# Sinkhorn on 128 partitions with a block matmul for the column sums, and float32 loading of one batch's values

## The chip, the cores and the metric

The kernel runs on one core of one Trainium2 chip. The metric is the device time of one execution, in microseconds (us). The kernel before takes 251.91 us (median of three runs, 251.24 to 252.35).

Engine names, as the profile has them: PE is TensorE (PEld is its weight load), DVE is VectorE, ACT is ScalarE, POOL is GpSimd, SP is SyncE. A "q" behind a name is that engine's sequencer, which issues transfers. Shapes in the profile are partitions x elements: the kernel's on-chip tiles have up to 128 rows, called partitions. Every instruction carries the line of the kernel's source, so the same operation has different line numbers in different kernels; the text says which is which.

## The reference

Two stages follow each other. The first is a block-sorted attention: four batches, eight heads, 768 positions, head dimension 64. The positions form eight blocks of 96. A small matrix for every batch and head is normalised by five Sinkhorn rounds and then mixes the blocks of the keys and of the values:

```python
P = sort_net                                   # (4, 8, 8, 8)
for _ in range(5):
    P = np.exp(P - P.max(-1, keepdims=True))
    P = P / (P.sum(-1, keepdims=True) + 1e-9)  # row sums
    P = P / (P.sum(-2, keepdims=True) + 1e-9)  # column sums
k_sorted = np.einsum('bhij,bhjcd->bhicd', P, k_blocks)
v_sorted = np.einsum('bhij,bhjcd->bhicd', P, v_blocks)
attn = softmax(q_block @ k_sorted_block.T / 8)      # inside each block
x    = attn @ v_sorted                              # -> (3072, 512)
```

The second stage is a gated feed-forward block on these 3072 rows, with weights of 512x1536, 512x1536 and 1536x512:

```python
out = (silu(x @ w_gate) * (x @ w_val)) @ w_out
```

## The kernel before

The feed-forward matmuls are the mass of the work, and they keep TensorE busy once batch 0's attention has delivered the first rows. Until then there is a start-up: Sinkhorn, value mixing ("tv"), key mixing ("tkq"), scores ("qk"), attention times values ("av_ps"), and then the first gate matmul ("g_ps"). The change and the argument touch this start-up.

```python
# loads: all of q, k, v on GpSimd, which casts float32 to bfloat16 on the way
load_v(0, 0, HC); load_v(0, HC, C)             # batch 0's values, two halves of columns
make_identity(nc, ident)
load_q(0, 0, C)
for lo, hi in ((0, 32), (32, 64), (64, 80), (80, 96)):
    load_k(0, lo, hi)
copy_v(nc.gpsimd, 0, lowr, 0)                  # transposing copies of the values into vch
copy_v(nc.gpsimd, 0, lowr, 3)
landed = const.tile([R, 1], BF16)
nc.gpsimd.tensor_copy(landed, kq_tiles[0][0:R, C - 1, D - 1:D])   # waits for the last key piece
# ... then the weight loads ...

# Sinkhorn on 32 partitions (batch, head) x 64 elements; all sums on DVE, Exp on ACT
for it in range(N_ITER):
    nc.scalar.activation(p_ps, p_sb if it == 0 else p_ps, AF.Exp)
    # ... it 2 and 3: one transposing value copy on ACT behind the Exp ...
    nc.vector.reduce_sum(rowred[:, :, 0], p_ps, axis=AX.X)
    nc.vector.reciprocal(rowred, rowred)
    nc.vector.tensor_mul(p_ps, p_ps, rowred.to_broadcast([BH, NB, NB]))
    nc.vector.reduce_sum(colred[:, 0, :], p_ps.transpose([0, 2, 1]), axis=AX.X)
    nc.vector.reciprocal(colred, colred)
    if it < N_ITER - 1:
        nc.vector.tensor_mul(p_ps, p_ps, colred.to_broadcast([BH, NB, NB]))
# ... two expansions to p_bf, then 16 small matmuls ("weights") spread P over 128 partitions ...
mix_of(0, w_ps)                                # masks it into vmix and rmix (bfloat16)

# filling matmuls keep TensorE active meanwhile; their results are not used
for _ in range(114): ...                       # 32 columns each
fill(idle_ps, 6)                               # 512 columns each, released by the first values
nc.tensor.matmul(idle_ps[0:NB, 0:NB], lhsT=hold, rhs=hold, ...)   # released by ACT in round five
fill(idle_ps, 5)

def v_chunk(b, at, n, eng, tag):               # value mixing
    ...
    for ld in range(n):
        nc.tensor.matmul(tp[:, ld, :], lhsT=vch[rows, col:col + 128], rhs=mix, start=True, stop=True)
    drain(eng, ...)
# 64 such matmuls, then 192 of key mixing (kq_chunk), then qk, av, transposes, gate
```

The softmax here doesn't subtract the row's maximum and nothing guards it: scores larger than these inputs give would overflow.

## Time and profile before

The first profile of the kernel before fell into a slow state (an execution far above the fastest of the same kernel). The second line below has each engine's busy time, share of the span and number of instructions, TensorE first. Page of the kernel before, first profile:

```profile
span 621.8 us, 6025 instructions
PE 606.0 (97%) x2542; PEld 269.0 (43%) x2568; DVE 165.1 (27%) x342; ACT 113.0 (18%) x187; POOL 51.6 (8%) x46
```

A span of 621.8 us is not that of the timed executions of 251.9; the profiled one took 623.76. The prediction had only this page. The unchanged kernel was therefore profiled again as the first experiment (b_again). From here on "before" means this profile. The page of the kernel before, profiled again; PEclk is the granted clock of TensorE in tenths, in 40 equal slices of the span:

```profile
span 250.0 us, 6051 instructions
PE 240.3 (96%) x2568; PEld 143.2 (57%) x2568; DVE 159.4 (64%) x342; ACT 110.7 (44%) x187; POOL 51.8 (21%) x46
PEclk9999999999999999999999999999999999999999
```

The same profile by stages. The columns are: stretch, its length, busy time of PE, PEld, DVE, ACT and POOL with instruction counts, then the granted clock, DMA share and GB/s:

```profile
0.00:12.70 12.70, 8.48 (x145) 5.09 (x146) 8.62 (x45) 8.23 (x12) 10.07 (x15) 1.00 0.81 157
12.70:20.50 7.80, 7.62 (x262) 6.01 (x263) 6.34 (x8) 5.38 (x8) 4.28 (x7) 1.00 0.69 103
20.50:25.30 4.80, 4.50 (x82) 2.93 (x83) 4.12 (x14) 3.94 (x8) 3.14 (x5) 1.00 1.27 159
25.30:250.00 224.70, 219.71 (x2080) 129.18 (x2079) 140.27 (x277) 93.11 (x161) 34.35 (x20) 1.00 0.50 91
```

The rows are Sinkhorn, mixing, scores and attention, and the dense part. A clock of 1.00 in the first row says little: time without a clock record counts as full, and the record starts at 8.29 us.

### The profile page before, as it was taken

Reading aid. Unit: us, or ns where it says so; the run is one execution under the profiler, and the core shown is the slowest. Engines: PE = TensorE matmul, PEld = TensorE weight load, DVE = VectorE, ACT = ScalarE, POOL = GpSimd, SP = SyncE. Lnnn points to the kernel's source line nnn. Section 1 sums busy time; section 2 is a strip of 40 time slices with the busy share of each in tenths; the row PEclk is TensorE's granted clock in tenths of the full one; section 3 lists DMA queues with packets and bytes.
Section 4 is the critical chain, followed back from the end, with each engine's and each line's share of the span. In section 5 each row is a group of like instructions: output and inputs, shape, how many; then the busy total and the mean of one; then the engine's idle time right before and its main releaser. Section 6 shows DMA issues by size and latency. Waiting matters only on the chain.

```text
span 621.8 us, 6025 instructions
## 1 busy us (share of the span) xinstructions
PE 606.0 (97%) x2542; PEld 269.0 (43%) x2568; DVE 165.1 (27%) x342; ACT 113.0 (18%) x187; POOL 51.6 (8%) x46
## 2 busy tenths in 40 slices
PE   7999999999999999999999999999999999999997
PEld 4754545544444444544434343334334433333323
DVE  5433333322332322223223122123113112212200
ACT  5331212121021111222102201102112111110100
POOL 6675000600000000000000000000000000000000
DMA  7999920000006000000100000001000000000001
GB/s 153 149 208 211 180 16 2 1 18 17 1 17 105 15 17 1 17 1 23 31 6 23 24 13 17 18 13 31 17 16 14 17 16 14 17 17 0 18 30 38
DMA packets 37866, 23.98 MB, mean 39 GB/s; under 512 B 26064, under 2 KB 34000, under 8 KB 37328
## 3 DMA queue, kind: packets, MB, share of 16 engines
q0 software_dynamic: 21328, 14.16, 15.5%
q1 hardware_dynamic: 16512, 9.45, 5.5%
q8 instruction: 20, 0.33, 0.2%
q14 instruction: 6, 0.05, 0.0%
HBM read 28.32 MB, written 7.86 MB: 58 GB/s over the span
## 4 chain that ended last, share of the span: by engine, by line
PE 97%; issue 2%; DVE 0%
PE v_ps L376 27%; PE g_ps L358 27%; PE o_ps L393 25%; PE tkq L237 3%; PE av_ps L307 3%; PE qk L280 2%; PE idle_ps L419 2%; PE tv L249 2%; PE tv L259 2%; PE x_ps L324 1%; PE o_ps L409 1%; PE idle_ps L422 1%; PE g_ps L506 1%; PE v_ps L506 0%; PE w_ps L435 0%
## 5 line engine op out<-in xcount | busy, mean ns | idle before, releaser
L376 PE MATMUL v_ps<-xt,wv_sb 128*128 128x384 bf16 x380 | 190.7, 686 | 0.0
L358 PE MATMUL g_ps<-xt,wg_sb 128*128 128x384 bf16 x376 | 188.9, 683 | 0.0
L393 PE MATMUL o_ps<-wo_sb,h 128*128 128x512 bf16 x255 | 161.3, 832 | 7.7 <-issue 7.7
L368 DVE SCALAR_TENSOR_TENSOR gs_sb<-th_sb,g_ps 128x384 bf16<-128x384 bf16 x96 | 52.9, 551 | 251.1 <-ACT th_sb L366 251.1
L358 PEld LDWEIGHTS <-wg_sb 128*128 128x128 bf16 x376 | 64.1, 176 | 86.9 <-issue 86.5
L376 PEld LDWEIGHTS <-wv_sb 128*128 128x128 bf16 x380 | 60.9, 165 | 93.5 <-issue 93.2
L366 ACT ACTIVATE th_sb<-g_ps 128x384 bf16<-128x384 f32 x96 | 47.2, 491 | 257.2 <-PE g_ps L358 252.4
L393 PEld LDWEIGHTS <-h 128*128 128x128 bf16 x276 | 47.1, 174 | 98.8 <-issue 98.7
L381 DVE SCALAR_TENSOR_TENSOR h<-v_ps,gs_sb 128x384 bf16<-128x384 f32 x96 | 52.5, 547 | 63.0 <-PE v_ps L376 62.9
L398 ACT COPY o_sb<-o_ps 128x512 f32<-128x512 f32 x23 | 13.5, 586 | 158.7 <-PE o_ps L393 158.7
L307 PEld LDWEIGHTS <-e_all 96*128 96x128 bf16 x256 | 26.2, 153 | 17.1 <-issue 16.5
L120 POOL COPY vch<-v 64x1536 bf16<-64x1536 bf16 (+1 forms) x10 | 27.7, 2807 | 57.4 <-PE tv L249 53.9
L307 PE MATMUL av_ps<-vt,e_all 96*128 96x65 bf16 x256 | 27.6, 287 | 0.3 <-PE x_ps L324 0.3
L293 ACT ACTIVATE e_all<-qk 96x768 bf16<-96x768 f32 x30 | 22.6, 802 | 28.7 <-PE qk L280 28.7
L313 DVE TENSOR_TENSOR st<-av_ps,r_sb 96x512 bf16<-96x512 f32 x32 | 21.7, 680 | 0.2
L311 DVE RECIPROCAL r_sb<-av_ps 96x8 f32<-96x8 f32 x32 | 6.5, 203 | 49.3 <-PE av_ps L307 49.3
L237 PE MATMUL tkq<-rmix,kq 128*64 128x64 bf16 x384 | 14.9, 271 | 1.0 <-issue 1.0
L237 PEld LDWEIGHTS <-kq 128*64 128x64 bf16 x384 | 13.7, 183 | 4.8 <-issue 4.7
L215 DVE CAST vt<-tv 96x1024 bf16<-96x1024 f32 (+1 forms) x9 | 9.9, 1105 | 14.1 <-PE tv L249 7.4
L419 PE MATMUL idle_ps<-warm_sb 128*128 128x512 bf16 x19 | 12.5, 795 | 0.7 <-issue 0.3
L217 ACT CAST vt<-tv 96x1024 bf16<-96x1024 f32 (+1 forms) x9 | 9.2, 1026 | 18.3 <-PE tv L259 11.7
L324 PEld LDWEIGHTS <-st 96*128 96x128 bf16 x64 | 8.8, 170 | 7.2 <-issue 7.2
(79 smaller groups left out, 200.2 us busy)
## 6 DMA issues: line engine op xcount, KB each, us to landing
out_dram<-o_sb SPq DMA_DIRECT2D x23, 256.0 KB, 2.0
v<-in_v_dram POOLq DMA_DIRECT2D x3, 768.0 KB, 19.6
kq<-in_q_dram POOLq DMA_DIRECT2D x2, 768.0 KB, 14.1
wg_sb<-in_moe_w_gate_dram POOLq DMA_DIRECT2D x6, 256.0 KB, 8.4
wv_sb<-in_moe_w_val_dram POOLq DMA_DIRECT2D x6, 256.0 KB, 9.1
wo_sb<-in_moe_w_out_dram POOLq DMA_DIRECT2D x1, 1536.0 KB, 25.3
kp<-in_k_dram POOLq DMA_DIRECT2D x2, 768.0 KB, 14.9
q_scr<-in_q_dram POOLq DMA_DIRECT2D x2, 768.0 KB, 28.6
```

What stands on the lines that cost most here:

```text
L120: eng.tensor_copy(dst, src.transpose([0, 2, 1]))
L237: nc.tensor.matmul(tp[two * D:(two + 1) * D, lc, :], lhsT=kq_tiles[b][:, at + lc, :], rhs=rm[:, two, :], start=True, stop=True)
L293: nc.scalar.activation(e_all[:, n:n + 2, 0:4 * C], wide[0:C, :, 0:4 * C], AF.Exp, scale=scale)
L307: nc.tensor.matmul(o[:, two, i4, :], lhsT=e[:, i4 * C:i4 * C + 128], rhs=vt[:, 2 * g + two, half * 4 + i4, :], start=True, stop=True)
L313: nc.vector.tensor_tensor(st.rearrange("p i two d -> p two i d"), o[0:C, :, :, 0:D], r_sb.to_broadcast([C, 2, 4, D]), op=ALU.mult)
L358: nc.tensor.matmul(g_ps, lhsT=wg_sb[:, kc, ts(m, 128)], rhs=xt[:, kc, :], start=(kc == 0), stop=(kc == NKC - 1))
L366: nc.scalar.activation(th_sb, g_ps, AF.Tanh, scale=0.5)
L368: nc.vector.scalar_tensor_tensor(gs_sb, th_sb, 1.0, g_ps, op0=ALU.add, op1=ALU.mult)
L376: nc.tensor.matmul(v_ps, lhsT=wv_sb[:, kc, ts(m, 128)], rhs=xt[:, kc, :], start=(kc == 0), stop=(kc == NKC - 1))
L381: nc.vector.scalar_tensor_tensor(h_tiles[n][:, m, :], v_ps, 0.5, gs_tiles.pop(m), op0=ALU.mult, op1=ALU.mult)
L393: nc.tensor.matmul(o_ps, lhsT=h_w[:, m, ts(t3, 128)], rhs=wo_sb[:, m, :], start=(m == 0), stop=(m == NFC - 1))
L419: nc.tensor.matmul(tile, lhsT=warm_sb[:, 0:128], rhs=warm_sb, start=True, stop=True)
```

## The change

The intent is to shorten the Sinkhorn chain and its end, and to take work off GpSimd:

1. P stands on 128 partitions (pair of batches, head, row) with 16 elements each. Row sums stay on DVE; column sums come from one float32 matmul with a block-diagonal matrix of ones.
2. The last round yields the mixing matrix through one multiply, two matmuls with a selection matrix, a reciprocal and one masked write, in place of two expansions, 16 matmuls and two masked writes. One matrix now serves values and keys; for this, batch 1's queries and keys swap halves of the partitions.
3. Batch 0's values come as float32 in four pieces on SyncE, not as a cast to bfloat16 on GpSimd. The transposing copies do the cast.
4. The weight loads wait for an earlier key piece.
5. Four units of batch 1 are transposed by DMA, not by PE.
6. The filling matmuls are arranged anew, around the block matmuls.

```diff
-    p_sb = const.tile([BH, NB, NB], FP32)
-    nc.sync.dma_start(out=p_sb, in_=sn)
+    p_sb = const.tile([128, NP, NB], FP32)
+    nc.scalar.dma_start(out=p_sb, in_=sn)
+    blk = const.tile([128, 128 // NB, NB], FP32)          # block-diagonal ones
@@
+    v0_tiles = []
+    for half in range(2):
+        t = kqp.tile([128, HC * D + 16], FP32, name=f"v0_{half}", tag="kqt")
+        t = t[0:H * NB, 0:HC * D].rearrange("p (c d) -> p c d", d=D)
+        for part in range(2):
+            c0 = half * HC + part * QC
+            nc.sync.dma_start(out=t[:, part * QC:(part + 1) * QC], in_=v_nat[0, :, c0:c0 + QC, :])
+        v0_tiles.append(t)
@@
-    load_v(0, 0, HC)
-    load_v(0, HC, C)
@@
-    copy_v(nc.gpsimd, 0, lowr, 0)
-    copy_v(nc.gpsimd, 0, lowr, 3)
+    copy_v0(nc.gpsimd, 0, 0, 24)
+    copy_v0(nc.gpsimd, 1, 20, 28, 0, 32)
+    copy_v0(nc.gpsimd, 1, 20, 28, 32, 32)
@@  the round
+        nc.scalar.activation(e_ps, p_sb if it == 0 else a_ps, AF.Exp)
+        # it 1, 2, 3: value copies on ACT, behind the Exp
+        nc.vector.reduce_sum(rows_sb[:, :, 0], e_ps, axis=AX.X)
+        nc.vector.reciprocal(rows_sb, rows_sb)
+        nc.vector.tensor_mul(x_sb, e_ps, rows_sb.to_broadcast([128, NP, NB]))       # float32
+        nc.tensor.matmul(c_ps..., lhsT=blk_flat, rhs=x_sb..., start=True, stop=True)
+        dots(32) if it < 2 else fill(idle_ps, 4)                                    # filling matmuls
+        nc.vector.reciprocal(c_ps, c_ps)
+        nc.vector.tensor_mul(a_ps, x_sb, c_ps)
@@  units of batch 1
-                if b < 2:
+                if b == 0 or b == 1 and u < H2:
```

(The fill and dots line is drawn together from four lines.)

## The prediction

> **What bounds the kernel now.** The only profile of before fell in a slow state: span 621.8 us against 251.9 us timed, PE busy 97% with a 384-column matmul every 0.43 to 0.50 us. I trust its DVE, ACT and DMA durations and rescale PE. [...]
>
> **Start-up, from the timeline of before.** Exp starts at 2.40 us; one Sinkhorn round is 1.7 us (six DVE ops 0.22 to 0.26 us apart, one Exp of 0.19). The chain ends at 10.9, two expansions reach 11.64, then come 16 small matmuls and one multiply (0.21). In the profile these matmuls wait behind slow warm-up matmuls until 13.87; at full clock I estimate the first value-mixing matmul at 12.7 us. It also needs the last ACT transposing copy, which ends at 12.61, so two paths are level.
>
> **What the change does.**
> 1. A round loses one reduction (0.24 us), its ops shrink from 64 to 16 elements (estimated 0.05 us each), but gains a float32 block matmul with two engine hops. I assume 0.4 us for it (nothing in this trace is float32): 1.7 to 1.9 us a round, no gain or a small loss. Exp may start 0.3 us later (finer load, issued on ACT before its table load).
> 2. The end is shorter: no expansions (0.74), no 16 matmuls, one mix instead of two. Instead: one multiply of 128 elements, matmul, reciprocal, mix: about 1.3 us after the last row sum against about 2.2.
> 3. Batch 0's values arrive as float32 on SyncE, freeing 1.19 us of GpSimd issue and letting copies start earlier; ACT has no copies after 11.5 us. I expect value mixing to start near 11.9 us: gain 0.8 us.
> 4. Weight loads no longer wait for the last key piece (before: 4.6 us wait, ending 16.63). They start perhaps 1 us earlier; not critical by itself, but it keeps the stream ahead (output weights land at 57 us in before).
> 5. Four units of batch 1 use DMA instead of PE transposes: 16 fewer. In the slow trace four take 0.43 us; at full clock I estimate 0.06 to 0.08 us each, about 1.1 us off the dense PE stage, plus four 0.36 us DVE copies that cost nothing. DMA transposes land in 2.3 us, well before use.
>
> **Sum.** 0.8 + 1.1 = about 2 us. Predicted 250.0 us; eight times in ten 248.0 to 251.9. Faster by over 2%: 0.06; within 2%: 0.92; slower: 0.02.
>
> **What would show it.** First value-mixing matmul at 11.5 to 12.3 us (before, in the same state, 12.7); 0.3 to 0.6 us between the DVE multiply and the next reciprocal; rounds of 1.7 to 1.9 us; ACT's last transposing copy before 11.6; weight issues starting near 15.5; 16 fewer PE transposes, four more DMA ones, PE not waiting for them.
>
> **What would make it wrong.** A float32 matmul well over 0.6 us, times five, would eat the gain. Warm-up matmuls before each block matmul could delay it if the clock is low, or thinner filling could leave PE slow during value and key mixing (cost 2 to 3 us). Float32 values landing late would block ACT's copies and, behind them, the next Exp. If start-up is bound by key loads rather than the chain, item 3 yields nothing.

Cut from the first paragraph is a TensorE rate that no trace had shown, with the split that rested on it: about 30 of the 252 us for a start-up in which PE waits, and dense PE work for the rest. The forecast's sum, 0.8 + 1.1 = about 2 us, loses no term by the cut.

## More of the kernel before

Timeline of the kernel before, in its start-up. Columns: start in us, duration, engine, line, operation, what it writes and reads, count; in brackets the idle time of the engine just ahead and what ended it:

```profile
6.09 5.62 POOL L120 COPY vch<-v 64x1536 bf16<-64x1536 bf16 x2 [0.48 <-DMA v<-in_v_dram]
7.73 0.19 ACT L187 ACTIVATE p_ps<-p_ps 32x64 f32<-32x64 f32 x1
9.40 0.19 ACT L187 ACTIVATE p_ps<-p_ps 32x64 f32<-32x64 f32 x1
9.61 2.97 ACT L118 COPY vch<-v 64x768 bf16<-64x768 bf16 x2
12.09 0.21 DVE L445 TENSOR_TENSOR vmix<-mask,w_ps 64x64 bf16<-64x64 bf16 x1 [0.53 <-PE w_ps L435]
12.72 2.02 PE L249 MATMUL tv<-vmix,vch 64*128 64x64 bf16 x64
14.73 1.33 PE L237 MATMUL tkq<-rmix,kq 128*64 128x64 bf16 x64
20.50 0.69 PE L280 MATMUL qk<-kqt 64*128 64x96 bf16 x24
25.26 0.48 PE L506 MATMUL g_ps<-xt,wg_sb 128*128 128x384 bf16 x2
```

Two Exp stand 9.40 − 7.73 = 1.67 us apart: that is one Sinkhorn round. Two paths end together: the mixing matrix is written from 12.09 on, and ACT's last value copy ends at 9.61 + 2.97 = 12.58. Value mixing starts at 12.72, behind both. The first gate matmul starts at 25.26; this is the number to watch.

## The result, and the profile after

The changed kernel takes 259.29 us (median of four runs, 259.03 to 259.89); the kernel before took 252.03 in the same rounds (251.24 to 252.35). The ratio is 1.0296, with a 95% interval of 1.0266 to 1.0327. A ratio here is the mean time of one kernel's fast runs over the mean of the other's fast runs of the same rounds, so it is not quite the ratio of the medians. The result is slower by more than 2%, outside the predicted range.

The page of the changed kernel, and then the stages:

```profile
span 257.0 us, 6031 instructions
PEclk9986999999999999999999999999999999999999
0.00:16.90 16.90, 9.81 (x151) 7.00 (x153) 7.23 (x42) 7.38 (x11) 8.65 (x16) 1.00 0.86 187
16.90:27.20 10.30, 9.40 (x259) 8.32 (x263) 6.43 (x8) 5.48 (x7) 9.56 (x13) 0.67 0.88 109
27.20:32.50 5.30, 4.28 (x81) 2.86 (x83) 3.65 (x11) 4.01 (x8) 2.23 (x5) 1.00 1.51 212
32.50:257.00 224.50, 217.95 (x2043) 128.71 (x2063) 139.29 (x273) 92.86 (x161) 31.57 (x16) 1.00 0.47 88
```

Read against the four stages of before, the whole loss lies ahead of the dense part: 4.2 us in the Sinkhorn stage (16.9 against 12.7), 2.5 in mixing (10.3 against 7.8, at a clock of 0.67), 0.5 behind it. The dense part takes 224.5 us against 224.7. (The four DMA transposes do save about 1 us there, but in this profile PE also stands idle for 1.06 us from 68.64 on, a stall of a kind that comes up again below.)

Timeline of the changed kernel, the lines that answer to those of before:

```profile
5.97 0.50 PEld L240 LDWEIGHTS chain<-x_sb,blk 128*128 128x128 f32 x2 [0.66 <-issue]
6.00 0.58 PE L240 MATMUL chain<-x_sb,blk 128*128 128x16 f32 x2 [0.58 <-DVE x_sb L239]
6.62 0.27 DVE L253 RECIPROCAL chain<-chain 128x16 f32<-128x16 f32 x1 [0.57 <-PE chain L240]
7.72 1.05 ACT L141 CAST vch<-v 64x512 bf16<-64x512 f32 x1 [2.48 <-DMA v<-in_v_dram]
8.68 0.16 ACT L227 ACTIVATE chain<-chain 128x16 f32<-128x16 f32 x1
10.79 0.17 ACT L227 ACTIVATE chain<-chain 128x16 f32<-128x16 f32 x1 [0.56 <-DVE chain L254]
12.91 0.17 ACT L227 ACTIVATE chain<-chain 128x16 f32<-128x16 f32 x1 [0.47 <-DVE chain L254]
14.55 0.28 DVE L266 SCALAR_TENSOR_TENSOR rmix<-f_ps,cinv,mask 64x64 bf16<-64x64 f32 x1
15.16 3.36 POOL L143 CAST vch<-v 64x896 bf16<-64x896 f32 x2 [6.53 <-DMA v<-in_v_dram]
16.89 3.57 PE L313 MATMUL tv<-rmix,vch 64*128 64x64 bf16 x64 [2.31 <-POOL vch L143]
20.39 1.92 PE L301 MATMUL tkq<-rmix,kq 128*64 128x64 bf16 x64
27.21 0.69 PE L344 MATMUL qk<-kqt 64*128 64x96 bf16 x24
32.47 0.48 PE L527 MATMUL g_ps<-xt,wg_sb 128*128 128x384 bf16 x2 [0.24 <-ACT xt L281]
```

Four things can be read from it.

- Value mixing waits for values. At 16.89 it starts after waiting 2.31 us for GpSimd's copies, and those began at 15.16 after waiting 6.53 us for the last piece of the load.
- The chain itself was held up by values. ACT's copy waited 2.48 us for a piece and began at 7.72. The Exp behind it in ACT's program had been released by DVE's result (ended at 7.10), but started only at 8.68.
- A round takes 2.12 us where nothing disturbs it (12.91 − 10.79), not 1.67. The float32 matmul appears as two matmuls with two weight loads.
- Value mixing takes 3.57 us, not 2.02, and the first 64 key-mixing matmuls 1.92, not 1.33. The clock record has half clock from 17.1 to 23.9 us; in before it is full from 8.3 us to the end.

The view of transfers, up to 20 us, has the load itself. Columns: what, issuing queue, count, KB each, median time from issue to landing. First before, then the changed kernel:

```profile
v<-in_v_dram POOLq DMA_DIRECT2D x2, 384.0 KB, 5.4
```

```profile
v<-in_v_dram SPq DMA_DIRECT2D x4, 384.0 KB, 6.8
```

The bytes written are twice as many. The trace's landing events are plainer than the medians: before, the two pieces land at 6.04 and 7.94 us; after, the four pieces land at 5.80, 7.69, 9.38 and **15.03**. The queries landed at 12.42 before and 14.68 after.

The records of the single packets show the sharing directly. In the changed kernel the values wrote 223 KB/us from 3.0 to 7.2 us, with no queries beside them. The first packet of the queries started at 7.20, when 80 of the values' 256 packets had not started. At the old rate these 80 would have ended near 9.4 us (an estimate: 80 x 6,144 bytes / 223 KB/us = 2.2 us); the last one ended at 13.68.

### The profile page after: what moved, and what is told of

It reads as the page before. It is cut to its first block, busy times and chain, and to the rows that moved or that the text cites. A ratio compares the mean times of both kernels' runs of the same rounds, so it can differ in the third digit from the quotient of the medians.

```text
span 257.0 us, 6031 instructions
## 1 busy us (share of the span) xinstructions
PE 241.4 (94%) x2532; PEld 146.9 (57%) x2558; DVE 156.6 (61%) x332; ACT 109.7 (43%) x186; POOL 52.0 (20%) x47
## 4 chain that ended last, share of the span: by engine, by line
PE 83%; DMA 5%; DVE 4%; issue 3%; ACT 2%; SPq 1%; POOL 1%; DVEq 0%; ACTq 0%; POOLq 0%
PE v_ps L440 23%; PE g_ps L422 22%; PE o_ps L457 22%; DMA v<-in_v_dram 5%; PE tkq L301 4%; PE av_ps L371 3%; PE qk L344 2%; PE tv L313 2%; PE tv L323 1%; DVE gs_sb L432 1%; DVE st L377 1%; PE o_ps L473 1%; ACT e_all L357 1%; DVE h L445 1%; PE x_ps L388 1%
## 5 line engine op out<-in xcount | busy, mean ns | idle before, releaser
L440 PE MATMUL v_ps<-xt,wv_sb 128*128 128x384 bf16 x380 | 77.3, 326 | 0.3
L422 PE MATMUL g_ps<-xt,wg_sb 128*128 128x384 bf16 x376 | 76.5, 325 | 0.0
L457 PE MATMUL o_ps<-wo_sb,h 128*128 128x512 bf16 x255 | 61.9, 379 | 1.2 <-issue 0.2
L440 PEld LDWEIGHTS <-wv_sb 128*128 128x128 bf16 x380 | 35.7, 97 | 24.1 <-issue 1.4
L422 PEld LDWEIGHTS <-wg_sb 128*128 128x128 bf16 x376 | 34.5, 97 | 22.7
L457 PEld LDWEIGHTS <-h 128*128 128x128 bf16 x276 | 26.2, 98 | 28.2
L371 PEld LDWEIGHTS <-e_all 96*128 96x128 bf16 x256 | 12.2, 98 | 5.0 <-ACT e_all L357 0.9
L371 PE MATMUL av_ps<-vt,e_all 96*128 96x65 bf16 x256 | 13.5, 194 | 0.3 <-ACT e_all L357 0.2
L279 DVE CAST kqt<-tkq 128x1024 bf16<-128x1024 f32 (+1 forms) x7 | 7.5, 1071 | 4.4 <-PE tkq L301 3.8
L281 ACT CAST kqt<-tkq 128x1024 bf16<-128x1024 f32 (+1 forms) x7 | 6.1, 891 | 8.1 <-PE tkq L301 8.1
```

The lines of the kernel that those rows point to most:

```text
L279: nc.vector.tensor_copy(dst, src)
L371: nc.tensor.matmul(o[:, two, i4, :], lhsT=e[:, i4 * C:i4 * C + 128], rhs=vt[:, 2 * g + two, half * 4 + i4, :], start=True, stop=True)
L422: nc.tensor.matmul(g_ps, lhsT=wg_sb[:, kc, ts(m, 128)], rhs=xt[:, kc, :], start=(kc == 0), stop=(kc == NKC - 1))
L440: nc.tensor.matmul(v_ps, lhsT=wv_sb[:, kc, ts(m, 128)], rhs=xt[:, kc, :], start=(kc == 0), stop=(kc == NKC - 1))
L457: nc.tensor.matmul(o_ps, lhsT=h_w[:, m, ts(t3, 128)], rhs=wo_sb[:, m, :], start=(m == 0), stop=(m == NFC - 1))
```

## The experiments

The theory: (T1) the float32 load lands late and holds up both the chain (through ACT) and value mixing; (T2) a float32 block matmul makes a round longer; (T3) mixing that starts late and behind thin filling runs at half clock. Rivals: (R1) the new chain alone is the loss, (R2) the half clock alone is, and for the load, several reasons why it is late.

### b_again: the kernel before, unchanged

> The kernel before, unchanged, for a profile in the fast state. If the theory holds (late float32 values cost the start-up), its first value-mixing matmul (tv) starts near 12.7 us, about 4 us before the 16.9 us of the changed kernel, and the first gate matmul of the dense stage comes 4 to 7 us before the changed kernel's 32.5 us. If the rival holds (the loss lies in the dense stage, for example in the moved transposes), both start within 1 us of each other.

It gave 252.1 us and a profile with a span of 250.0 us: first gate matmul at 25.26 us, value mixing at 12.72. So they start 7.2 and 4.2 us earlier than in the changed kernel: the loss lies in the start-up, and the comparison above rests on this profile.

### v_bf16: the changed kernel with the values as before

```diff
-            nc.sync.dma_start(out=t[:, part * QC:(part + 1) * QC], in_=v_nat[0, :, c0:c0 + QC, :])   # and its tiles
+    load_v(0, 0, HC)
+    load_v(0, HC, C)                                # bfloat16 by cast, GpSimd, ahead of q and k
```

> The changed kernel with batch 0's values loaded as in the kernel before: cast to bf16, on GpSimd, ahead of queries and keys; all else as changed. Theory (float32 values on SyncE land late, both because they write twice the bytes and because they share the DMA engines with the queries): values land by 7.2 us, tv starts near 13.3 us, total 250.5 to 252.5. Rival (the new Sinkhorn rounds of 2.1 us against 1.7 and their float32 matmuls are what costs 7 us): it stays above 256.

It took 254.65 us, ratio 1.0088 (1.0017 to 1.0159; one of its four runs, 257.99, was slow). The load's pieces landed at 6.58 and 8.40. Timeline of v_bf16:

```profile
6.63 6.14 POOL L135 COPY vch<-v 64x1536 bf16<-64x1536 bf16 x3
13.91 2.24 PE L307 MATMUL tv<-rmix,vch 64*128 64x64 bf16 x64 [0.40 <-DVE fin L269]
16.08 1.92 PE L295 MATMUL tkq<-rmix,kq 128*64 128x64 bf16 x64
27.78 0.48 PE L521 MATMUL g_ps<-xt,wg_sb 128*128 128x384 bf16 x2 [0.24 <-ACT xt L275]
```

GpSimd's copies are done at 12.8, and value mixing waits for DVE (the chain), not for values. Of the 7.2 us by which the first gate matmul was late, the cast load takes away 32.47 − 27.78 = 4.7, a shorter spell of half clock included (15.5 to 18.9 us, where the changed kernel had 17.1 to 23.9). The other 2.5 remain: longer rounds, and that shorter spell. So neither R1 nor R2 is the whole.

### v_only: the kernel before with only the float32 load

```diff
-    load_v(0, 0, HC)
-    load_v(0, HC, C)
+            nc.sync.dma_start(out=t[:, part * QC:(part + 1) * QC], in_=v_nat[0, :, c0:c0 + QC, :])   # float32, four pieces
```

> The kernel before with only the values' load moved to SyncE as float32. Theory: last value piece lands at 13 to 15 us, tv starts at 16 to 17 us, total 256 to 259. Rival (new Sinkhorn costs): total within 1.5 us of before, 252.

(The value copies read the new pieces, so the split of columns between ACT and GpSimd moves a little, and the filling matmul that reads values is float32.) It took 263.46 us, ratio 1.0455 (1.0401 to 1.0508): in the expected direction, but a miss in size. The load alone, in the old chain, costs more than the whole change. Timeline of v_only:

```profile
13.30 1.48 ACT L136 CAST vch<-v 64x768 bf16<-64x768 f32 x1 [7.19 <-DMA v<-in_v_dram]
14.69 0.20 ACT L202 ACTIVATE p_ps<-p_ps 32x64 f32<-32x64 f32 x1
21.62 3.59 PE L264 MATMUL tv<-vmix,vch 64*128 64x64 bf16 x64 [0.75 <-POOL vch L138]
```

With the old order of loads the queries are issued at 1.47 us (2.74 in the changed kernel), so that their packets run beside the values' from 4.08 on, and the second piece lands only at 13.28. ACT's copy waits 7.19 us, and the Exp that stood at 7.73 in before follows at 14.69. A value copy ahead of an Exp on the same engine turns a late load into a late chain. The clock record is half from 11.6 to 28.6.

### v_f32_gp: the changed kernel, float32 values, but ahead of the queries in the same queue

```diff
-            nc.sync.dma_start(out=t[:, part * QC:(part + 1) * QC], in_=v_nat[0, :, c0:c0 + QC, :])
+            nc.gpsimd.dma_start(out=t[:, part * QC:(part + 1) * QC], in_=v_nat[0, :, c0:c0 + QC, :])
```

> The changed kernel with the values still float32, but issued on GpSimd ahead of queries and keys, so that nothing shares the engines with them. If sharing with the queries made them late, they land near 10 us (1.57 MB at the 209 KB/us that the trace shows for them alone) and tv starts near 14.5 us: total 255 to 257. If a float32 load is slow in itself whatever the queue, they land near 15 us and the total stays at 259. If only the sharing mattered and bytes did not, they land by 7.5 us and the total is 251 to 253.

It took 257.35 us, ratio 1.0196 (1.0141 to 1.0251). The pieces landed at 6.55, 8.45, 10.35 and 12.12: one piece of 393 KB in 1.9 us, or 207 KB/us. With the values ahead of the queries the last piece is 15.03 − 12.12 = 2.9 us earlier; against the cast's 7.94 it is still 4.2 us late (3.7 against the 8.40 of v_bf16). So the lateness has two parts, size and sharing. The division is rough: the queries' packets start at 9.92 here, when 17 of the values' 256 had not started, so a little sharing is left in the 4.2. The landing was expected near 10 us, a miss, and value mixing started at 16.73, not 14.5, a further one: GpSimd built the block matrix later, behind four issues of its own, and the first block matmul came at 4.62 (3.88 in the changed kernel); ACT's copy still waited 2.45 us; and this line of the timeline of v_f32_gp shows a new cost on DVE:

```profile
12.38 1.60 DVE L252 COPY rmix<-ident 64x64 bf16<-64x64 bf16 x1
```

The same copy takes 0.18 us in the changed kernel. GpSimd's copy of values (12.24 to 15.57) ran beside it. DVE's copy took 1.60 us here, 1.11 and 0.64 us in v_bf16_mm16 and v_bf16, also beside GpSimd's copies, and in all three it ended 0.04 or 0.05 us after a copy of GpSimd's had ended. What ties the two together no run shows.

### after_warm: more filling ahead of value mixing

```diff
+    fill(idle_ps, 10)
     v_chunk(0, 0, 8, "v", "gen")
```

> The changed kernel with ten more 512-column warm-up matmuls on zeros between its last Sinkhorn matmul (ends 14.6 us) and its first value-mixing matmul (16.9 us), where PE stood idle for 2.3 us. Theory: that idle stretch is why the clock is granted at half from 17.0 to 23.8 us; with it filled the clock stays full, the stretch from the first tv to the first qk matmul falls from 10.3 us to 7.8 to 8.3 us, and the total falls by about 2.2 us, to 256.5 to 257.5. Rival (mixing is slow for another reason, as late keys or drains): the stretch stays above 9.5 us and the total at 259.

It took 258.45 us, ratio 1.0265 (1.0234 to 1.0295), a miss. The clock was not yet up, so ten filling matmuls ran at half speed (0.43 us each) and pushed value mixing to 19.25. From 19.6 us on the clock was full, and value mixing took 2.18 us and the first 64 key-mixing matmuls 1.33 (3.57 and 1.92 in the changed kernel). The stretch from the first tv to the first qk matmul was 9.0 us (10.3), with a stall of 1.07 us in it that new_shift takes up. So T3's size per matmul is right, but the filling has to come before, not in the way.

### b_nofill: the kernel before with thin filling

```diff
-    fill(idle_ps, 6)
     nc.tensor.matmul(idle_ps[0:NB, 0:NB], lhsT=hold, rhs=hold, start=True, stop=True)
-    fill(idle_ps, 5)
```

> The kernel before without its eleven 512-column warm-up matmuls during the Sinkhorn chain (loads, copies and chain untouched). If a half clock during the mixing is worth the 2.5 us by which the changed kernel's stretch from first tv to first qk matmul is longer (10.3 against 7.8 us), then here the clock record shows half speed during the mixing, tv still starts near 12.6 us, the stretch grows to 9.5 to 10.5 us, and the total to 253.5 to 254.8. If the clock does not matter there, stretch and total stay (7.8; 252).

It took 254.6 us, ratio 1.0086 (1.0045 to 1.0128), a hit but for value mixing, which started at 13.13 and not near 12.6. Timeline of b_nofill:

```profile
13.13 3.59 PE L249 MATMUL tv<-vmix,vch 64*128 64x64 bf16 x64
23.23 0.69 PE L280 MATMUL qk<-kqt 64*128 64x96 bf16 x24
```

From value mixing to the first score took 10.1 us, against 7.8, with half clock from 9.4 to 19.6. So taking filling alone away costs 2.3 us of mixing in the old kernel, nearly the 2.5 of the changed kernel's mixing stage.

The half-clock spells recorded in start-ups here last 3.41 us (v_bf16, among others), 6.83 (the changed kernel, new_shift), 10.24 (b_nofill) and 17.07 (v_only): one, two, three and five times 3.41. What ends a spell no run tests by itself.

### v_bf16_mm16: v_bf16 with a bfloat16 block matmul

```diff
-    blk = const.tile([128, 128 // NB, NB], FP32)
+    blk = const.tile([128, 128 // NB, NB], BF16)
-    x_sb = const.tile([128, NP, NB], FP32)
+    x_sb = const.tile([128, NP, NB], BF16)
```

> The variant with early bf16 values (254.3 us) with the block matrix and the row-normalised values of the Sinkhorn rounds in bf16, so that a round's column sum is one bf16 matmul where the float32 one ran as two. Theory (a round of 2.12 us where 1.7 to 1.9 was predicted is the float32 matmul, 0.76 us from multiply to reciprocal): a round falls to 1.7 to 1.85 us, the chain's end comes 1.2 us earlier, total 252.8 to 253.6. Rival (the hops between engines cost it, not float32): a round stays above 2.0 us.

It took 253.82 us, ratio 1.0066 (1.003 to 1.0101). The mechanism was a hit: undisturbed rounds took 1.64 and 1.68 us, not 2.12, each block matmul was one matmul, not two, and from DVE's multiply to the reciprocal passed 0.29 us, not 0.76. The total missed slightly (252.8 to 253.6 expected; one of the four runs, 256.96, was slow): ACT's copy again waited for values ahead of an Exp (6.85 to 7.81), and half clock came at 15.7 to 19.1. T2 holds. The output still agreed with the reference.

### b_4iter: a shorter chain in the kernel before

```diff
-    N_ITER = 5
+    N_ITER = 4                     # wrong on purpose
```

> Wrong result on purpose: the kernel before with four Sinkhorn rounds instead of five, so the chain ends 1.7 us earlier. If the transposing value copies (end 12.6 us) bind the start of the value mixing as much as the chain does, tv starts at 12.2 to 12.6 us and the total gains 0 to 0.4 us: then no faster Sinkhorn could have paid. If the chain alone binds, tv starts near 11.0 us and the total falls by 1.5 us, to 250.4.

It took 252.37 us, ratio 1.0014 (0.9955 to 1.0073), a hit. Timeline of b_4iter:

```profile
10.42 0.21 DVE L445 TENSOR_TENSOR vmix<-mask,w_ps 64x64 bf16<-64x64 bf16 x1 [0.53 <-PE w_ps L435]
12.46 2.69 PE L249 MATMUL tv<-vmix,vch 64*128 64x64 bf16 x64 [1.54 <-ACT vch L118]
```

The chain ended 1.67 us earlier, but value mixing started at 12.46, not 12.72, having waited 1.54 us for ACT's value copies. (The total is no clean measure: behind that wait this profile has half clock from 13.6 to 17.0 us, and the first gate matmul came at 25.99.) In the kernel before the chain and the copies are level, so no faster Sinkhorn could have paid by itself. (The check against the reference did not catch the missing round; the kernel is wrong all the same.)

### b_xdma: only the four DMA transposes

```diff
-                if b < 2:
+                if b == 0 or b == 1 and u < H2:
```

> The kernel before with only the four units of batch 1 moved from PE to DMA transposes. The prediction said 1.1 us less: 250.6 to 251.0, ratio 0.995 to 0.997. The trace of the changed kernel, whose loss at the end of the start-up (7.2 us) is nearly its whole loss (7.0 us of span), says at most 0.4 us: ratio 0.998 to 1.000.

It took 250.77 us, ratio 0.9957 (0.9935 to 0.9978, five rounds), a hit. Start-up was as before (first gate matmul at 25.25), and the span 249.1 against 250.0. This item of the change pays about 1 us, and the version beats both kernels.

### new_mended: the change with its start-up mended

The values by cast on GpSimd, a bfloat16 block matmul, large filling matmuls in every round and four ahead of value mixing, ACT's copies only from the third Exp on, DVE's small copy earlier.

```diff
@@ on top of v_bf16_mm16
-        if it == 1:
-            copy_v0(nc.scalar, 0, 24, 8)           # ACT's copies moved to it 2, it 3 and behind the loop
-        if it < 2: dots(32)
-        else:      fill(idle_ps, 4)
+        fill(idle_ps, 3 if it < 2 else 4)
@@
+    fill(idle_ps, 4)
     v_chunk(0, 0, 8, "v", "gen")
```

> The changed kernel with its three faults mended at once: values early, cast, ahead of queries and keys on GpSimd; bf16 block matmul in the rounds; warm-up of three to four 512-column matmuls in every round, ACT's value copies no sooner than the third Exp, and the small DVE copy moved away from GpSimd's copies. If these are the whole cause, tv starts at 12.8 to 13.4 us, the clock is full from about 9 us, the stretch from tv to qk is 7.8 to 8.2 us, and the total is 251.0 to 251.8 (about 0.9 us over the 250.8 of before with DMA transposes alone). If something else of the change costs, it stays above 253.

It took 255.28 us, ratio 1.0136 (1.0075 to 1.0196): a clear miss, and the most useful one. Value mixing started at 12.43, earlier than in before, at full clock. Then key mixing stalled. Timeline of new_mended, TensorE alone:

```profile
12.43 2.02 PE L301 MATMUL tv<-rmix,vch 64*128 64x64 bf16 x64 [0.16 <-issue]
17.58 0.95 PE L289 MATMUL tkq<-rmix,kq 128*64 128x64 bf16 x48 [1.49 <-ACT kqt L269]
19.73 0.92 PE L289 MATMUL tkq<-rmix,kq 128*64 128x64 bf16 x46
23.50 0.22 PE L289 MATMUL tkq<-rmix,kq 128*64 128x64 bf16 x2 [2.86 <-issue]
```

PE stopped for 2.86 us between two matmuls of one chunk, with nothing that it waited for ("issue"), and for 1.49 us earlier; there ACT, which the line names, had been done at 16.81. Half clock followed from 23.7 to 27.1, and the first gate matmul came at 30.24. What these stalls were is taken up in new_shift.

### probe_load: how fast a load goes into 64 and into 128 partitions

Four loads of batch 0's values late in b_xdma, one at a time on GpSimd's queue; behind each, a GpSimd copy of one column waits for the landing, and nothing else uses them:

```diff
+    for n, (dtype, rows, src) in enumerate(((FP32, 64, v_64), (FP32, 128, v_128), (BF16, 64, v_64), (BF16, 128, v_128))):
+        probe = vnp.tile([128, C * D // (2 if dtype is FP32 else 1)], dtype, name=f"probe{n}", tag="vn")
+        nc.gpsimd.dma_start(out=probe[0:rows, 0:half], in_=src)
```

> Before with DMA transposes, plus four loads of batch 0's values on GpSimd one after the other late in the kernel, into a dead tile: float32 into 64 partitions (0.79 MB), float32 into 128 partitions (1.57 MB), bf16 by cast into 64 partitions (0.39 MB written), bf16 by cast into 128 partitions (0.79 MB written). If bytes written are what limits a load (209 KB/us), they take about 3.8, 7.5, 1.9 and 3.8 us plus some 2 us each. If the 64 partitions halve the rate, float32 into 128 partitions takes about 3.8 us plus 2. If the cast costs nothing and bytes read limit, the two casts take as long as the float32 loads of the same rows.

The time from issue to landing (6.5, 8.0, 6.3 and 7.8 us) did not separate the theories, because 1.5 to 3.8 us of each lie outside of its packets. The records of the single packets do. Every packet read 12,288 bytes of float32:

```
load                       packets   bytes written each   median time of one    KB written per us
float32, 64 partitions        64          12,288                946 ns                189
float32, 128 partitions      128          12,288                460 ns                378
cast,    64 partitions        64           6,144                474 ns                131
cast,    128 partitions      128           6,144                474 ns                127
```

The last column runs from the first packet's start to the last one's end. A float32 load into 64 partitions goes at half the rate of one into 128 (189 against 378), while a cast goes at 131 and 127. Why, no run tests; a cast writes only half of the bytes that it reads (6,144 of 12,288). In the start-up, with 6,144 bytes written, a packet took about 475 ns in either kernel (median 478 before, 466 after), and the float32 load has 256 of them where the cast has 128: that is what its size costs. That 128 partitions would have cured it in this kernel is not shown: no run loads the values so.

### v_split: float32 values, half of them to the other 64 partitions

```diff
-        t = t[0:H * NB, 0:HC * D].rearrange("p (c d) -> p c d", d=D)
+        t = t[half * R:half * R + R, 0:HC * D].rearrange("p (c d) -> p c d", d=D)
-            nc.sync.dma_start(out=t[:, part * QC:(part + 1) * QC], ...)
+            (nc.sync, nc.scalar)[half].dma_start(out=t[:, part * QC:(part + 1) * QC], ...)
```

> Edit: the changed kernel, values of batch 0 still float32, but the second half of their columns is loaded to partitions 64 to 127 on ScalarE's queue, while the first half goes to partitions 0 to 63 on SyncE's; the copies read them there. The result stays right. Theory A, the late values are a matter of partitions: in the last run float32 packets of 12,288 bytes took 946 ns (median) into 64 partitions and 460 ns into 128, while casts took 474 ns into either, so a load into 64 partitions moves at half the rate of its source side, and the float32 load needs twice the time of the cast of the same values only because of that. With both halves of the partitions in use at once, the 1.57 MB take about 4.2 us at 378 KB/us from 2.9 us on: the last piece lands at 7.5 to 8.5 us (15.03 in the changed kernel), before the queries' packets start in earnest; value mixing starts at 13.9 to 14.6 us (16.9; Exp may start 0.5 us later behind ScalarE's two more issues), first gate matmul at 27.8 to 28.6, ratio to before 1.007 to 1.014, about 254.5 us. Rival B, two transfers to the two halves of the partitions run one after the other[...]: the last piece lands at 11.5 to 15 us, value mixing at 16.5 or later, ratio 1.02 to 1.03.

It took 258.64 us, ratio 1.0278 (1.0259 to 1.0298); the profiled execution, 261.08, was the longest of the six. Theory A failed and rival B held: the pieces landed at 6.24, 7.99, 11.20 and 15.25 us, and value mixing started at 18.68. While both loads ran (4.0 to 8.9 us; the second one's first packet of values starts at 3.91) they wrote 232 KB/us, against 214 in v_f32_gp in the same stretch and 223 in the changed kernel before its queries start: 4 to 9% more, not twice as much. At 9 us all but 13 of the 256 packets had started; the last ones then stood among the packets of queries and keys, until 13.6 us. Of the loads tried here, only the one transfer over 128 partitions (probe_load) wrote 378 KB/us, and a few late packets are enough to make a piece late.

### new_shift: new_mended with 104 more TensorE instructions ahead of mixing

Counted from zero, the two stalls of new_mended stand behind the recorded TensorE instructions 448 and 704 (matmuls and weight loads), 256 apart. In the packet records, transfers of kind "instruction" of 16,384 bytes run beside them; how many instructions one holds no trace shows. In new_mended the first of these fetches starts at 15.32 us and the next at 21.00, after the second stall had begun; in before they start at 8.25, 15.72 and 21.56. after_warm, too, has a stall (1.07 us from 24.53 on) behind number 704. The traces hold more of this. In all profiles but the slow one I find six such waits of TensorE in key mixing, of about 0.8 us or more: these three, one in v_only, also behind number 704, one in v_bf16 at 64.0 us and the one in the changed kernel at 68.6. Each ended 1.3 to 1.6 us after the end of the last such packet. In before and b_xdma TensorE came to number 704 1.5 and 1.4 us after that packet's end and did not wait: they stood on the edge. To test it, the count was changed:

```diff
-        fill(idle_ps, 3 if it < 2 else 4)
+        fill(idle_ps, 2 if it < 2 else 3)
+        dots(14)                       # 32 columns each
```

> Edit: new_mended, with one filling matmul of 512 columns in each of the first four rounds replaced by 14 filling matmuls of 32 columns, about the same TensorE time but 104 more instructions ahead of the mixing. In new_mended the two stalls of key mixing stand exactly 256 recorded TensorE instructions apart (after the 448th and the 704th), a fetch of 16,384 bytes of instructions lands about then, and in the kernel before the fetches came 104 to 117 instructions later in the count, without a stall. Theory A, TensorE waited for instruction fetch: the fetches move as in the kernel before (near 8, 15.5 and 21.5 us), no stall over 1 us is left between 12.4 us and the first gate matmul, which starts at 24.8 to 26.0 us (30.24); total 250.3 to 252.0 us, ratio 0.993 to 1.000. Rival B, the stalls come from drains, data or clock: stalls of over 1 us stay in key mixing, first gate matmul at 29 us or later, ratio 1.008 to 1.016.

It took 251.56 us, ratio 0.9976 (0.9894 to 1.0058): theory A, a hit on the total. The fetches start at 9.01, 16.69 and 24.32 us, and no stall of over 1 us is left between value mixing and the gate. (Counted at its start, the first fetch stands at number 416 in new_mended and the fetches of before that answer to both stalls at 534 and 869, so they came 118 and 164 instructions later, not "104 to 117".) The first gate matmul was at 27.42, later than expected, because this execution had half clock from 11.5 to 18.3; the four runs lie from 250.1 us (clock 1.0) to 253.7 (clock 0.98).

### new_dense: the filling put back, the count kept

```diff
-        fill(idle_ps, 2 if it < 2 else 3)
+        fill(idle_ps, (2, 3, 4, 4)[it])
         dots(14)
```

> Edit: new_shift with the 512-column filling matmuls of rounds two to four back (3, 4, 4 beside the 14 small ones each). Theory A, the spread of new_shift is the half clock before value mixing, which thin filling lets happen: with denser filling the clock is at full speed from about 7 us on with no half spell after it in most executions, value mixing takes about 2.0 us and not 3.6, the first gate matmul starts at 24.5 to 25.5 us (27.42), executions lie within 1.5 us of each other at 249.5 to 250.8 us, ratio 0.990 to 0.996. Rival B, the clock falls back whatever the filling of the rounds, for instance over the wait of key mixing or of the final matmuls: executions still spread over 2 us or more, ratio 0.995 to 1.003.

(The count grows by no more than 6.) It took 251.05 us (median of six runs, 250.19 to 251.70), ratio 0.9964 (0.9925 to 1.0002). Timeline of new_dense:

```profile
12.30 2.02 PE L302 MATMUL tv<-rmix,vch 64*128 64x64 bf16 x64
14.30 1.33 PE L290 MATMUL tkq<-rmix,kq 128*64 128x64 bf16 x64
20.05 0.69 PE L333 MATMUL qk<-kqt 64*128 64x96 bf16 x24
24.80 0.48 PE L517 MATMUL g_ps<-xt,wg_sb 128*128 128x384 bf16 x2
```

The clock is full from 7.6 us on, no stall is left (number 704 comes 1.5 us after its packet, on the edge again), and the first gate matmul starts at 24.80, against 25.26 in before and 32.47 in the changed kernel. The start-up was as theory A expected, and the runs lie 1.5 us apart; the median is 0.25 us above the expected interval and the ratio just above its edge. This kernel keeps the 128-partition Sinkhorn, the short end and the DMA transposes of the change. Mending the load, the block matmul's type, the filling and the instruction count gives back all of the 7 us. Its ratio against before includes 1.0, so it is no proven gain, and b_xdma, which alone is proven, gains as much. What is left of the new chain's lead is small: the mixing matrix is written from 11.25 on (12.09 before), but ACT's last value copy ends at 12.20 and the filling at 12.14, so mixing starts only 0.4 us earlier than before.

## Why the prediction was wrong

The prediction was 250.0 us (248.0 to 251.9); the result is 259.29. Point by point:

- **What bounds the kernel.** Right in kind: a start-up of 25.3 us (the estimate was about 30) and 224.7 us of dense TensorE work. Value mixing at 12.7 us was right to the tenth (12.72). The rate of TensorE, which no trace had shown by then, can be read from the fast profile (b_again): matmuls of 384 and 512 columns start 162 and 216 ns apart (medians).
- **Item 1, the round.** Mis-sized. "0.4 us" was assumed for the block matmul with its two hops; the trace has 0.77 us from the end of DVE's multiply (5.68 + 0.17 = 5.85) to the reciprocal (6.62), and the float32 matmul in it runs as two, 0.58 us together. A round takes 2.12 us, not 1.7 to 1.9. v_bf16_mm16 shows it: in bfloat16 0.29 us (0.19 to 0.22 the one matmul), and rounds of 1.64 and 1.68. The "0.05 us each" for smaller operations was close for DVE's multiplies (0.17 and 0.18 us, 0.22 before) and row sum (0.17, 0.21 before), but the second reciprocal grew to 0.27 from 0.19.
- **Item 2, the end.** From the last row sum (13.11) to the mixing matrix (14.55 + 0.28 = 14.83) takes 1.7 us, where 1.3 was predicted; the old end took 2.8 (9.62 to 12.43), where 2.2 was. Both terms were sized too small, but their difference, 1.1 us, is close to the predicted 0.9.
- **Item 3, the step that failed.** The prediction said that "Batch 0's values arrive as float32 on SyncE, freeing 1.19 us of GpSimd issue and letting copies start earlier", and expected value mixing "near 11.9 us: gain 0.8 us". In its place the last piece landed at 15.03 us against 7.94, and value mixing started at 16.89. The prediction counted an issue that became free and gave no time to the transfer itself. The load writes 1.57 MB, not 0.79, into the same 64 partitions, in twice as many packets of the same time (256 of 466 ns, median, against 128 of 478; in probe_load float32 went at 189 KB/us there against 378 into 128 partitions), which costs some 4.2 us (12.12 against 7.94, v_f32_gp); and on a queue of its own it no longer stands ahead of the queries: their packets run beside its own from 7.20 us on, which costs the other 2.9 or more (15.03 against 12.12).
- **Even without the load there was little to gain.** b_4iter shows the chain and ACT's copies level in the kernel before.
- **Item 4.** Wrong: weights were issued from 18.59 us, later than before (16.35), not near 15.5, since all loads had slipped and GpSimd's late copies stood ahead.
- **Item 5.** Right: "about 1.1 us"; b_xdma gains 1.1 us (0.4%). Four PE transposes take 0.34 us at full clock in the changed kernel, and PE's busy time in transposes is 4.0 us in b_xdma (48 of them) against 5.3 in before (64).
- **The named risks.** One came true in full: late values that block ACT's copies and the next Exp (7.10 to 8.68). The slow PE in mixing came with the size that was named for it (2 to 3 us, 2.5 measured), but "thinner filling" is only part of its cause: PE also stood idle for 2.31 us ahead of it, waiting for values, and with early values and the same filling (v_bf16) the half clock lasts 3.4 us and not 6.8. One more came true in part, the float32 matmul. They were listed as risks, and all of "slower" was given 2%.

The sum of the loss at the first gate matmul, 7.2 us: 4.7 vanish with the cast load (v_bf16), and the other 2.5 and more vanish with a bfloat16 block matmul, denser filling and a moved instruction count (new_dense). How these last three divide the 2.5 us was not separated to the tenth. That the stalls are instruction fetch rests on their places in the count (448 and 704 in new_mended, 704 in after_warm and v_only), on the packets' times (the same 1.3 to 1.6 us in all six) and on new_shift; new_shift's edit also changed the clock's course, so a second reason for their disappearance is not excluded. Why the fetch came late in new_mended was not shown.

## What to carry to other kernels

When a load moves to another queue or another type, cost the transfer and not its issue: here bytes written (4.2 us late by size, v_f32_gp), the partitions they go to (189 against 378 KB/us in float32, probe_load), and what runs beside it (2.9 us more in the changed kernel). Do not put a copy that waits for a load ahead of a link of the critical chain on the same engine: in v_only a copy on ACT waited 7.19 us, and the Exp behind it came at 14.69 us in place of 7.73. And re-profile a start-up like this one after each edit: a change of filling alone cost 2 us in b_nofill, more than one round of the chain that it surrounds.
